# The second MoE weights cast in flight by GpSimd's DMAs, a last store in two halves, and a new order of the work

## The chip, the cores and the metric

The kernel runs on one core of a Trainium2 chip. Its time is the device time of one execution in microseconds (us). The engines that matter: TensorE (PE; PEld are its weight loads), VectorE (DVE), ScalarE (ACT), GpSimd (POOL) and SyncE (SP). In the kernel before, SP issues every DMA. Each engine works through its own instructions in program order and waits on semaphores for the others.

## The reference

The reference is a recurrent attention (RWKV-6) followed by a two-layer MoE block with a squared ReLU, all in float32:

```python
batch, n_heads, seq, head_dim = (4, 8, 768, 48)
for t in range(S):
    cur = einsum('bhd,bhe->bhde', u[None] * kt, vt)
    y[:, :, t] = einsum('bhd,bhde->bhe', rt, state + cur)
    state = wt[:, :, :, None] * state + einsum('bhd,bhe->bhde', kt, vt)
x = y.transpose(0, 2, 1, 3).reshape(3072, 384)
h = x @ w_in            # w_in: 384 x 2048
g = maximum(h, 0) ** 2
out = g @ w_out         # w_out: 2048 x 384
```

## The kernel before, in words

The 4 x 768 tokens are worked in 12 steps of 256 tokens (`T`), three for each batch entry. A step loads its w, r, k and v (384 KB each, `load_step`, line 200), turns the recurrence inside the step into matrix products, carries the state from step to step (`ts_`, `sn_`), and passes its 256 rows through the MoE.

A step s runs like this. `ww_` multiplies neighbouring decays, `lw_` takes logarithms, `cum_` sums them with triangular matmuls into PSUM, `exp_` and `ac_` exponentiate. `rw_` and `kw_` multiply r and k by w, and `rd_` scales them by the decays. `tr_` with `rkt_` (TensorE and a copy) or `dtr_` (a transposing DMA from SP) transposes the result. `p_` forms the products of r and k, `pm_` masks them. `su_` forms the update of the state. `y_`, `yc_` and `yq_` sum three parts of the output in one PSUM bank pair; the last uses `vq_`, made by `ku_`, `qp_` and `vq_` on POOL with `q_` on DVE between. `ysb_` copies the sum, `yt_` with `xt_` (or `dyt_` by DMA) transposes it. `m1_.s.g` is one of eight groups of six matmuls with the first weights; each fills one of four PSUM banks, which `rl_.s.g` (ReLU) reads and frees. `sq_.s.q` squares a quarter of the hidden rows. In steps 0 to 4 `m2_.s.c.q` multiplies a quarter with the second weights, four matmuls a group, and `os_` scales the result out. In steps 5 to 11 a scheme with seven instead of eight block products takes its place: `tw_` forms sums of weight blocks, `sw_` sums of hidden blocks, `pw_.s.1` to `pw_.s.7` are eight matmuls each, `cx_` and `ow_` gather them, and `store` writes 128 rows of the output.

The order of all this isn't made by loops: the string `ORDER` (line 17) lists every operation of all steps as one sequence of words, and the loop at line 634 issues them. Each engine gets its own operations in that order. A word such as `rl_.0.3=V` also says which engine takes it (A is ACT, V is DVE, G is POOL), and `:2` which PSUM bank. So `ORDER` fixes each engine's queue and SP's queue of DMAs too. Which SBUF buffer an operation uses follows from the order as well (`buf`, line 173): a buffer is handed on after a counted number of uses.

The MoE weights come as float32 and are used as float16. `load_wi(g)` and `load_wo(g)` (lines 208 and 213), called by the words `ld.g.i` and `ld.g.o`, let SP load a quarter (768 KB) into one of four staging buffers `w_st`, and `cast` (line 218) copies it into `wi_sb` or `wo_sb`. Quarter q of the second weights is what `m2_.s.c.q` multiplies with; quarter g of the first serves the groups `m1_.s.2g` and `m1_.s.2g+1`. Each staging buffer carries one quarter of the first and one of the second weights; after its last use it becomes output buffers, room for the weight sums, or room for the hidden sums (lines 183 to 191).

Of the kernel before, what the change touches and what calls it, by code (L numbers as in the profile page):

```python
# [22 lines left out]
pm_.1.1 cast.i.1=A yt_.0:3 sn_.0.1 su_.1:0 xt_.0=V qp_.1 ts_.1.0=V m1_.0.1:3 cast.i.2=A pm_.1.0 m1_.0.3:2 m1_.0.0:0  # L23
rl_.0.1=A sn_.1.0 q_.1 ld.2.v cast.i.3=A m1_.0.2:1 rl_.0.3=V m1_.0.4:3 vq_.1 ld.0.o ts_.1.1=V rl_.0.2=A y_.1:1
rl_.0.0=V yc_.1 ld.3.k ww_.2=G yq_.1 m1_.0.5:2 ysb_.1=V ku_.2 m1_.0.6:0 lw_.2 rl_.0.4=V rl_.0.5=A yt_.1:1 sq_.0.0=A
cum_.2:1 ld.1.o xt_.1=V m1_.0.7:3 ld.3.w kw_.2=G rl_.0.6=A m1_.1.1:1 ld.2.o exp_.2 sn_.1.1 m1_.1.4:2 rl_.1.1=V
rl_.0.7=A m1_.1.0:0 rw_.2=G sq_.0.3=A rl_.1.4=V m1_.1.5:1 rl_.1.0=V qp_.2 m1_.1.7:2 rd_.2.0 rl_.1.5=A m1_.1.6:0 ld.3.r
rl_.1.7=A rd_.2.1 tr_.2.0:3 cast.o.0=G rl_.1.6=A m1_.1.2:1 ld.3.o rkt_.2.0=V v_.2=A tr_.2.1:2 rl_.1.2=A m1_.1.3:0
ku_.3 rkt_.2.1=V ac_.2 sq_.1.0=A su_.2:0 q_.2 m2_.0.0.0:1 ld.4.w m2_.0.1.0:3 ts_.2.0=V sq_.0.1=A cast.o.1=G rl_.1.3=V
ld.3.v p_.2.0:1 p_.2.1:0 ww_.3=V sq_.1.1=A m2_.1.1.0:0 vq_.2 m2_.1.0.0:2 pm_.2.1 lw_.3 sq_.1.2=A m2_.0.0.1 pm_.2.0  # L30
m2_.1.1.1 sn_.2.0 sq_.1.3=A m2_.1.0.1 sq_.0.2=V cast.o.2=A m2_.0.1.1 ld.4.k qp_.3 y_.2:1 yc_.2 yq_.2 m2_.1.1.2 kw_.3=G
ld.4.r q_.3 cast.o.3=A cum_.3:0 m2_.0.1.2 ysb_.2=V ww_.4=G m2_.0.0.2 exp_.3 m2_.1.0.2 ac_.3 rw_.3=G lw_.4 rd_.3.1
m2_.1.1.3 v_.3=G m2_.1.0.3 os_.1.1=V dtr_.3.1 cum_.4:1 rd_.3.0 kw_.4=G os_.1.0=A yt_.2:0 exp_.4 m2_.0.0.3 xt_.2=V
ku_.4 dtr_.3.0 ac_.4 m2_.0.1.3 os_.0.0=A rw_.4=V su_.3:0 store.0.0 m1_.2.4:1 ts_.3.0=A ld.4.v rd_.4.1 m1_.2.7:0
# [63 lines left out]
def kernel(  # L98
# [54 lines left out]
    for kind, first in (("r", 0), ("k", 16)):  # L153
# [8 lines left out]
                xT=9, gt=20, o=2, sg=8, xz=6)  # L162
    live, done = {}, {}
    in_halves = {int(word.split(".")[1]) for word in ORDER.split() if word.startswith("rd_.") and word.count(".") == 3}

    def uses_of(kind, key):
        if kind == "S":
            s, c = key
# [443 lines left out]
    def store(s, c):  # L612
        t0 = s * T + c * C
        nc.sync.dma_start(out=out[t0:t0 + C, :], in_=buf("o", s, c)[:])
# [61 lines left out]
```

## Time and profile before

| | us |
|---|---|
| median of 3 runs | 178.47 (177.96 to 178.54) |
| the profiled execution, its own time | 177.58 |
| its span in the profile | 175.8 |
| busy in the span: PE, DVE, ACT, POOL | 169.0, 141.8, 135.4, 125.5 |

The profile is one execution; its times count from the start of the span, and 1.8 us of the execution's time lie outside the span. A row of the timeline gives start, length, engine, line of the code, operation, what it writes `<-` what it reads, shapes and types, and, where the engine stood idle before it, for how long and what released it in brackets. A row of the groups gives the busy time, the mean length in ns of one instruction, and the idle time before them. A row of the stretches gives the busy time of each engine between two times. For a DMA a row gives how long its issue took and the time from issue to landing. A DMA's line is that of its issue: L201 is a load of w, r, k or v, L209 of the first and L214 of the second weights, L614 a store.

### The profile page before, as it was taken

The page shows a single profiled execution, that of the slowest core. Times are in us where ns is not written, and L with a number is a line of the kernel's source. Part 1 is how long each engine was busy: PE and PEld are TensorE (multiplying, and loading weights), DVE is VectorE, ACT ScalarE, POOL GpSimd, SP SyncE. Part 2 cuts the span into 40 slices and gives each one's busy share as a digit, 9 for nine tenths or more (in the row PEclk, how much of TensorE's full clock was granted, in tenths as well). Part 3 has the DMA queues.
Part 4 walks back from the last instruction along what each step waited for, and adds up shares of the span by engine and source line. Part 5 has one row for each costly group of instructions (what it writes and reads, how often), then busy time and mean ns, then how long its engine had stood idle before and what let it go on. Part 6 is the DMA issues. An engine that isn't in the chain of part 4 may idle for free.

```text
span 175.8 us, 5827 instructions
## 1 busy us (share of the span) xinstructions
PE 169.0 (96%) x2431; PEld 133.7 (76%) x2431; DVE 141.8 (81%) x221; ACT 135.4 (77%) x229; POOL 125.5 (71%) x116
## 2 busy tenths in 40 slices
PE   7978899999999999999999999999999999999992
PEld 2346778756686786578876888899988888989991
DVE  5499977996968859987987979969899879788640
ACT  6779798997569878759899799997896778467220
POOL 6398999999597399959999239679948764264320
PEclk9999999999999999999999999999999999999999
DMA  5999999999579999597998969949969710420133
GB/s 148 323 360 383 360 248 365 355 349 260 108 200 316 232 228 265 144 212 195 296 186 224 335 132 246 229 106 303 175 133 158 192 45 4 147 77 4 45 117 111
DMA packets 82523, 36.55 MB, mean 208 GB/s; under 512 B 75841, under 2 KB 80962, under 8 KB 82498
## 3 DMA queue, kind: packets, MB, share of 16 engines
q1 hardware_dynamic: 82498, 36.19, 81.1%
q8 instruction: 19, 0.31, 0.7%
q14 instruction: 6, 0.05, 0.1%
HBM read 25.17 MB, written 4.72 MB: 170 GB/s over the span
## 4 chain that ended last, share of the span: by engine, by line
PE 85%; SPq 5%; DMA 5%; issue 1%; ACT 1%; ACTq 0%
PE one L513 35%; PE one L590 19%; PE one L536 15%; PE att L450 7%; DMA w_st_b<-in_moe_w_in_dram 5%; SPq L201 4%; PE att L404 3%; PE att L426 2%; SPq L209 1%; PE att L334 1%; PE one L496 1%; PE att L336 1%; PE one L379 1%; PE att L332 0%; ACT gt_b L520 0%
## 5 line engine op out<-in xcount | busy, mean ns | idle before, releaser
L513 PE MATMUL one<-xT_b,wi_sb 128*128 128x256 bf16 x576 | 70.2, 273 | 0.5 <-ACT gt_b L520 0.3
L513 PEld LDWEIGHTS <-wi_sb 128*128 128x128 f16 x576 | 54.8, 98 | 9.1 <-issue 1.3
L520 ACT ACTIVATE gt_b<-one 128x512 f16<-128x512 f32 x70 | 40.9, 596 | 10.2 <-PE one L513 9.3
L528 ACT ACTIVATE gt_b<-gt_b 128x1024 bf16<-128x1024 f16 x42 | 43.5, 1056 | 1.4 <-DVE gt_b L522 1.0
L415 DVE TENSOR_TENSOR pmT_b<-att,mask 128x1024 bf16<-128x1024 f32 x22 | 26.3, 1219 | 4.4 <-PE att L404 4.4
L536 PE MATMUL one<-wo_sb,gt_b 128*128 128x384 f16 x160 | 28.7, 326 | 0.0
L590 PEld LDWEIGHTS <-gt_b 128*128 128x128 bf16 x280 | 23.2, 98 | 0.9 <-issue 0.4
L307 POOL TENSOR_TENSOR ku_b<-k_b,u_bc 128x768 f32<-128x768 f32 x12 | 22.0, 1831 | 0.6 <-ACT u_bc L238 0.5
L536 PEld LDWEIGHTS <-gt_b 128*128 128x128 bf16 x160 | 15.1, 98 | 9.6 <-issue 0.5
L312 POOL TENSOR_TENSOR ku_b<-ku_b,r_b 128x768 f32<-128x768 f32 x12 | 22.0, 1831 | 0.2
L440 POOL TENSOR_TENSOR S_b<-t_b,ac_buf 128x384 bf16<-128x384 f32 x20 | 16.8, 841 | 6.1 <-ACT t_b L434 5.4
L522 DVE TENSOR_SCALAR gt_b<-one 128x512 f16<-128x512 f32 x26 | 17.6, 687 | 2.8 <-PE one L513 1.8
L318 POOL TENSOR_TENSOR vq_b<-v_b,q_b 128x768 bf16<-128x768 f32 x12 | 18.2, 1518 | 0.7 <-DVE q_b L315 0.6
L590 PE MATMUL one<-wo_sb,gt_b 128*128 128x192 f16 x168 | 16.2, 246 | 0.0
L370 DVE TENSOR_TENSOR rdec_buf<-r_b,att 128x768 bf16<-128x768 f32 x12 | 11.4, 949 | 2.4 <-POOL r_b L300 1.2
L370 DVE TENSOR_TENSOR rdec_buf<-k_b,att 128x768 bf16<-128x768 f32 x12 | 11.4, 949 | 1.9 <-ACT ac_buf L356 1.5
L595 ACT ACTIVATE w_st_b<-one 128x192 f32<-128x192 f32 x14 | 4.4, 329 | 10.3 <-PE one L590 10.2
L300 POOL TENSOR_TENSOR r_b<-r_b,w_b 128x384 f32<-128x384 f32 x8 | 8.0, 1002 | 5.2 <-DMA r_b<-in_r_dram 5.2
L315 DVE TENSOR_REDUCE q_b<-ku_b 128x16 f32<-128x768 f32 x12 | 11.3, 943 | 0.0
L590 PE MATMUL one<-w_st_b,gt_b 128*128 128x192 f16 x112 | 11.2, 246 | 0.0
L436 DVE TENSOR_TENSOR t_b<-S_b,att 128x384 f32<-128x384 bf16 x16 | 8.8, 549 | 3.0 <-POOL S_b L440 2.5
L288 POOL TENSOR_TENSOR ww_b<-w_b 128x384 f32<-128x384 f32 x7 | 8.1, 1159 | 4.0 <-DMA w_b<-in_w_dram 4.0
(100 smaller groups left out, 268.2 us busy)
## 6 DMA issues: line engine op xcount, KB each, us to landing
w_b<-in_w_dram SPq DMA_DIRECT2D x12, 384.0 KB, 5.7
r_b<-in_r_dram SPq DMA_DIRECT2D x12, 384.0 KB, 5.3
k_b<-in_k_dram SPq DMA_DIRECT2D x12, 384.0 KB, 4.9
v_b<-in_v_dram SPq DMA_DIRECT2D x12, 384.0 KB, 4.6
out_dram<-w_st_b SPq DMA_DIRECT2D x24, 192.0 KB, 2.1
w_st_b<-in_moe_w_in_dram SPq DMA_DIRECT2D x4, 768.0 KB, 8.3
w_st_b<-in_moe_w_out_dram SPq DMA_DIRECT2D x4, 768.0 KB, 8.2
rkT_b<-rdec_buf SPq DMA_TRANSPOSE x18, 3.4
```

Source lines behind the costliest of these rows:

```text
L307: nc.gpsimd.tensor_mul(buf("ku", s)[:], buf("k", s)[:, :, 1:3, :], u_bc[:, :, None, :].to_broadcast([C, H, 2, D]))
L312: nc.gpsimd.tensor_mul(ku[:], ku[:], buf("r", s)[:, :, 0:2, :])
L318: nc.gpsimd.tensor_mul(buf("vq", s)[:].rearrange("p j h d -> p h j d"), buf("v", s)[:], buf("q", s)[:, :, :, None].to_broadcast([C, H, 2, D]))
L370: nc.vector.tensor_mul(rdec[:, i, :, heads, 0:D], x.rearrange("p h j d -> p j h d"), decay[:, None, :, :].to_broadcast([C, 2, n, D]))
L415: nc.vector.tensor_mul(pmT, ps_p[:].rearrange("p e (a x) -> p (e a) x", a=2), mk.to_broadcast([C, 4, 2 * C]))
L440: nc.gpsimd.tensor_mul(buf("S", s + c, 1 - c)[:], buf("t", s, c)[:].rearrange("p (a e d) -> p a e d", a=HP, e=2), tiles["a_c", s][:, :, c, ...
L513: nc.tensor.matmul(ps1[:, j, :], wi_sb[:, n // 4, kk, n % 4 * 128:(n % 4 + 1) * 128], xT[:, :, kk, :], start=(kk == 0), stop=(kk == KT - 1))
L520: nc.scalar.activation(rl, m1, AF.Relu, scale=RS)
L522: nc.vector.tensor_scalar(out=rl, in0=m1, scalar1=RS, scalar2=0.0, op0=ALU.mult, op1=ALU.max)
L528: nc.scalar.activation(gt, rl, AF.Square)
L536: nc.tensor.matmul(m2, gt[:, n, c * C:(c + 1) * C], wo_sb[:, n, :], start=(n == 0), stop=(n == NT - 1))
L590: nc.tensor.matmul(where_to, gt[:, n, :], wo[:, n, :], start=(n == 0 and i in (1, 2, 5)), stop=(n == NT // 2 - 1), skip_group_check=True)
```

## The change

- The second weights are no longer loaded by SP into staging buffers and cast by POOL and ACT. A new operation `gld_(g)` issues from GpSimd's queue a DMA that reads a quarter of the float32 weights from DRAM and writes it as float16 straight into `wo_sb`. There are four of them. The four words `ld.g.o` and the four words `cast.o.g` are gone.
- The staging buffers carry the first weights alone, so they become output buffers and room for sums after one use each (`done` counts 1 to 4 instead of 5 to 8).
- `store` can write one half of the columns. The last store, 11.1, goes as two, `store.11.1.1` (the right half) ahead of store 11.0 and `store.11.1.0` behind it.
- One dummy matmul at the very end (`warm_.1.5`) is gone.
- `ORDER` is new from the first MoE matmul on: the sequence on every engine, the PSUM banks, and for 108 operations the engine. Up to `m1_.0.1` it is unchanged.

The order's part up to step 2, its end, and the code (words that the lists share are on both sides):

```diff
-pm_.1.1 cast.i.1=A yt_.0:3 sn_.0.1 su_.1:0 xt_.0=V qp_.1 ts_.1.0=V m1_.0.1:3 cast.i.2=A pm_.1.0 m1_.0.3:2 m1_.0.0:0
-rl_.0.1=A sn_.1.0 q_.1 ld.2.v cast.i.3=A m1_.0.2:1 rl_.0.3=V m1_.0.4:3 vq_.1 ld.0.o ts_.1.1=V rl_.0.2=A y_.1:1
-rl_.0.0=V yc_.1 ld.3.k ww_.2=G yq_.1 m1_.0.5:2 ysb_.1=V ku_.2 m1_.0.6:0 lw_.2 rl_.0.4=V rl_.0.5=A yt_.1:1 sq_.0.0=A
-cum_.2:1 ld.1.o xt_.1=V m1_.0.7:3 ld.3.w kw_.2=G rl_.0.6=A m1_.1.1:1 ld.2.o exp_.2 sn_.1.1 m1_.1.4:2 rl_.1.1=V
-rl_.0.7=A m1_.1.0:0 rw_.2=G sq_.0.3=A rl_.1.4=V m1_.1.5:1 rl_.1.0=V qp_.2 m1_.1.7:2 rd_.2.0 rl_.1.5=A m1_.1.6:0 ld.3.r
-rl_.1.7=A rd_.2.1 tr_.2.0:3 cast.o.0=G rl_.1.6=A m1_.1.2:1 ld.3.o rkt_.2.0=V v_.2=A tr_.2.1:2 rl_.1.2=A m1_.1.3:0
-ku_.3 rkt_.2.1=V ac_.2 sq_.1.0=A su_.2:0 q_.2 m2_.0.0.0:1 ld.4.w m2_.0.1.0:3 ts_.2.0=V sq_.0.1=A cast.o.1=G rl_.1.3=V
-ld.3.v p_.2.0:1 p_.2.1:0 ww_.3=V sq_.1.1=A m2_.1.1.0:0 vq_.2 m2_.1.0.0:2 pm_.2.1 lw_.3 sq_.1.2=A m2_.0.0.1 pm_.2.0
...
-ow_.11.4=V pw_.11.4 ow_.11.2=V store.11.0 warm_.1.5 ow_.11.3=A store.11.1
+pm_.1.1 cast.i.1=A yt_.0:3 sn_.0.1 su_.1:0 xt_.0=V qp_.1 ts_.1.0=V m1_.0.1:3 cast.i.2=A pm_.1.0 m1_.0.2:0 m1_.0.0:1
+rl_.0.1=A sn_.1.0 q_.1 ld.3.w cast.i.3=A m1_.0.5:2 y_.1:1 vq_.1 ld.2.v ww_.2=V m1_.0.3:3 yc_.1 rl_.0.3=A ld.3.k gld_.0
+yq_.1 rl_.0.0=V lw_.2 m1_.0.4:3 ysb_.1=A ts_.1.1=V m1_.0.7:1 gld_.1 rl_.0.5=V rl_.0.4=A cum_.2:1 rl_.0.7=A ld.4.w
+yt_.1:2 rw_.2=V gld_.2 rl_.0.2=A m1_.0.6:1 xt_.1=V exp_.2 ld.3.r m1_.1.3:3 kw_.2=G rl_.0.6=A rd_.2.0 m1_.1.1:2
+rl_.1.3=A sn_.1.1 m1_.1.6:0 rd_.2.1 rl_.1.1=A m1_.1.0:3 gld_.3 ld.3.v rl_.1.6=V tr_.2.0:1 rl_.1.0=A m1_.1.2:2 v_.2=G
+ld.4.k rkt_.2.0=V sq_.0.1=A m1_.1.7:0 ww_.3=G sq_.1.0=A tr_.2.1:1 rl_.1.7=V m1_.1.4:3 ku_.2 rkt_.2.1=V rl_.1.2=A
+su_.2:0 sq_.0.0=A rl_.1.4=V m1_.1.5:2 ts_.2.0=V m2_.1.1.0:0 qp_.2 rl_.1.5=A m2_.0.1.0:3 ac_.2 sq_.1.1=A m2_.0.1.1
+ku_.3 m2_.0.0.0:1 sq_.0.3=A q_.2 ld.4.r m2_.1.0.0:2 kw_.3=V sq_.1.2=A p_.2.0:1 p_.2.1:0 sn_.2.0 m2_.0.0.1 sq_.0.2=A
+pm_.2.0 m2_.1.1.1 sq_.1.3=A pm_.2.1 m2_.1.0.1 ld.4.v qp_.3 lw_.3 m2_.0.0.2 cum_.3:0 m2_.1.0.2 exp_.3 rw_.3=G m2_.1.1.2
+rd_.3.1 m2_.1.0.3 vq_.2 rd_.3.0 v_.3=A m2_.1.1.3 dtr_.3.1 y_.2:1 q_.3 ww_.4=G ac_.3 yq_.2 yc_.2 os_.1.1=V su_.3:0
...
+pw_.11.3 ow_.11.4=V store.11.1.1 pw_.11.4 ow_.11.2=V store.11.0 ow_.11.3=A store.11.1.0
...
+    in_parts = {tuple(int(x) for x in word.split(".")[1:3]) for word in ORDER.split()
+                if word.startswith("store.") and word.count(".") == 3}
...
+        more += kind == "o" and key in in_parts
...
-            if kind == "w_st" and done[kind] == 5:
+            if kind == "w_st" and done[kind] == 1:
...
-            elif kind == "w_st" and done[kind] in (6, 7):
+            elif kind == "w_st" and done[kind] in (2, 3):
...
-            elif kind == "w_st" and done[kind] == 8:
+            elif kind == "w_st" and done[kind] == 4:
...
-    def load_wo(g):
-        nc.sync.dma_start(
-            out=buf("w_st", "o", g)[:].rearrange("p (a d) -> p a d", d=DM),
+    def gld_(g):
+        nc.gpsimd.dma_start(
+            out=wo_sb[:, g * 4:(g + 1) * 4, :],
             in_=moe_w_out[g * 512:(g + 1) * 512, :].rearrange("(a p) d -> p a d", p=128))
...
-    def store(s, c):
-        t0 = s * T + c * C
-        nc.sync.dma_start(out=out[t0:t0 + C, :], in_=buf("o", s, c)[:])
+    def store(s, c, i=None):
+        t0, cols = s * T + c * C, slice(0, DM) if i is None else half[i]
+        nc.sync.dma_start(out=out[t0:t0 + C, cols], in_=buf("o", s, c)[:, cols])
```

## The prediction

> **What bounds the kernel now.** I read the busy time by stretch first, then the chain that ended last, and then the timeline of the start and the tail, because the first two show that nothing between start and tail can give anything.
>
> ```profile
> 19.00:24.00 5.00, 4.67 (x82) 3.79 (x81) 4.18 (x6) 4.01 (x5) 4.46 (x4) 1.00 1.02 292
> 24.00:172.00 148.00, 148.00 (x2135) 121.28 (x2132) 123.47 (x191) 116.53 (x198) 107.34 (x87) 1.00 0.80 195
> ```
>
> The rows give length, then busy time (instructions) of PE, weight load, DVE, ACT, POOL, then the granted clock, the DMA share and GB/s. From 24 to 172 us TensorE is busy 148.0 of 148 us at clock 1.00. Busy time alone doesn't show that it runs at its pace, so I look at the chain (start, length, what):
>
> ```profile
> 59.97 0.65 PE one L513 x6
> 60.62 0.65 PE one L536 x4
> ...
> 65.09 0.57 PE att L404 x32
> 65.67 0.76 PE one L513 x6
> ...
> 158.45 13.88 PE one L590 x168
> ```
>
> Six matmuls of 256 columns take 0.65, and 168 of 192 columns take 13.88 with no gap. The only loss that repeats is 0.10-0.11 us: the same six take 0.76 after the attention matmuls that use 64 rows. So the end is set by three things: when TensorE starts on the MoE (about 19 us), its work with these switches, and the 3.5 us from the last matmul at 172.3 to the end. The new order holds the same matmuls but one dummy at the end, so the 148 us can only grow: every wait put ahead of TensorE there is paid in full, and there are no waits to win back.
>
> **The change, part by part.** The sum is made against the profiled execution (177.58 us, span 175.8) and carried to the median of the runs, 178.47, which is 0.9 above it.
>
> *Casts and engines.* Two casts of 1.46 leave POOL and two leave ACT; 108 operations change between ACT, DVE and POOL. I cost that at nothing: beside TensorE's 148.0 us the row has DVE 123.5, ACT 116.5 and POOL 107.3, so TensorE's work covers them, as long as no single one comes late.
>
> *Switches.* Counting in the two orders how often TensorE goes from 128-row work into a group of 64-row work after its first MoE matmul, I get 26 before and 28 after: 2 x 0.10 = +0.2.
>
> *The start.* Up to the first MoE matmul the orders are equal, so these rows still hold:
>
> ```profile
> 19.04 2.78 PE L513 MATMUL one<-xT_b,wi_sb 128*128 128x256 bf16 x24 [0.20 <-DVE xT_b L500]
> 22.10 0.82 PE L513 MATMUL one<-xT_b,wi_sb 128*128 128x256 bf16 x6 [0.29 <-ACT gt_b L520]
> ...
> 26.19 4.75 PE L513 MATMUL one<-xT_b,wi_sb 128*128 128x256 bf16 x42
> ```
>
> ```profile
> 20.08 1.47 ACT L221 CAST wi_sb<-w_st_b 128x1536 f16<-128x1536 f32 x1 [0.89 <-DMA w_st_b<-in_moe_w_in_dram]
> ```
>
> Before, four groups of six run from 19.04 and the fifth waits 0.29 until 22.10. After, the fourth group is `m1_.0.5`, which needs the third cast of the first weights, done at 20.08 + 1.47 = 21.55; it starts at 21.6 and ends at 22.26, 0.16 later than the same amount of work before. With one of the two extra switches (`m1_.0.3` now splits `y_.1` from `yc_.1`), TensorE is through step 0 at 26.19 + 0.66 + 0.26 = 27.1 instead of 26.85.
>
> The next group needs `xt_.1` on DVE, and DVE's queue is where the change bites: `ww_.2` and `rw_.2` now stand on it, ahead of `xt_.1`, and both wait for loads.
>
> ```profile
> 20.58 0.94 DVE L315 TENSOR_REDUCE q_b<-ku_b 128x16 f32<-128x768 f32 x1
> ...
> 26.03 0.56 DVE L500 COPY xT_b<-one 128x768 bf16<-128x768 bf16 x1 [0.25 <-PE one L496]
> ```
>
> ```profile
> 21.60 1.47 POOL L318 TENSOR_TENSOR vq_b<-v_b,q_b 128x768 bf16<-128x768 f32 x1 [0.32 <-DVE q_b L315]
> 23.29 1.00 POOL L288 TENSOR_TENSOR ww_b<-w_b 128x384 f32<-128x384 f32 x1 [0.21 <-DMA w_b<-in_w_dram]
> ```
>
> ```profile
> L522 DVE TENSOR_SCALAR gt_b<-one 128x512 f16<-128x512 f32 x26 | 17.6, 687 | 2.8 <-PE one L513 1.8 <-ACT gt_b L520 0.6
> L436 DVE TENSOR_TENSOR t_b<-S_b,att 128x384 f32<-128x384 bf16 x16 | 8.8, 549 | 3.0 <-POOL S_b L440 2.5 <-PE att L426 0.5
> L300 DVE TENSOR_TENSOR r_b<-r_b,w_b 128x384 f32<-128x384 f32 x4 | 3.2, 808 | 0.5 <-DMA r_b<-in_r_dram 0.5
> L288 DVE TENSOR_TENSOR ww_b<-w_b 128x384 f32<-128x384 f32 x5 | 2.8, 556 | 1.0 <-DMA w_b<-in_w_dram 1.0
> ```
>
> DVE is free at 21.52 and waits for w of step 2, whose landing released POOL at 23.29. Then 23.29 + 0.56 (`ww_.2`) + 0.69 (`rl_.0.0`) + 0.55 (`ts_.1.1`) + 0.69 (`rl_.0.5`) = 25.8; `rw_.2` 0.81 makes 26.6, `xt_.1` 0.56 makes 27.15: TensorE, ready at 27.1, waits 0.1 at most. Behind `rw_.2` on DVE stand `xt_.1` and with it all of step 1's matmuls, so any lateness of r of step 2 after 25.8 is TensorE's.
>
> *That load, and the new queue.* Landings (k and r of step 2, from issue):
>
> ```profile
> L201 SPq DMA_DIRECT2D k_b<-in_k_dram x1: 4342/4342/4342, 13.6 to 13.6; - x1
> DMA to landing us min/median/max: 10.7/10.7/10.7
> L201 SPq DMA_DIRECT2D r_b<-in_r_dram x1: 3968/3968/3968, 18.0 to 18.0; - x1
> DMA to landing us min/median/max: 7.6/7.6/7.6
> ```
>
> k lands at 24.3 and r at 25.6, so r's transfer fills 1.3 us; the DMA share in 19-24 is 1.02, nothing is spare. Before, the second weights stand behind these loads in SP's one queue:
>
> ```profile
> q1 hardware_dynamic: 82498, 36.19, 81.1%
> ```
>
> ```profile
> L201 SPq DMA_DIRECT2D v_b<-in_v_dram x1: 1082/1082/1082, 22.0 to 22.0; - x1
> DMA to landing us min/median/max: 5.8/5.8/5.8
> L214 SPq DMA_DIRECT2D w_st_b<-in_moe_w_out_dram x4: 1022/2034/2256, 23.2 to 31.3; - x4
> DMA to landing us min/median/max: 6.7/8.2/8.3
> ```
>
> After, `gld_.0` comes from POOL once `vq_.1` ends at 23.07. (The least values, 1.02 and 6.7, are the first weight load's.) What POOL pays for an issue no row shows; the nearest are these issues of the same transfers from SP, 1.02 for the first and up to 2.26 for those behind a full queue. POOL's queue is its own and empty, so I take 1.1, and keep nothing and 2.26 as the ends. The Trainium skill (DMA: Bandwidth & Descriptors, Specifications) gives about 1 us to the first byte for a DMA issued from GpSimd, which would leave the sum as it is. So the weights start at 24.2, beside r. How two queues share the engines no row shows either: from no delay (r first) to all of the first weights first. I take half each: r needs 2.6 instead of 1.3 us, lands at 26.9, and DVE's `rw_.2` starts 1.1 later than 25.8: +1.1.
>
> *POOL's own queue.* Before, `vq_.2` ends at 35.22 + 1.79 = 37.0 and is used at 40.46.
>
> ```profile
> 28.87 1.81 POOL L312 TENSOR_TENSOR ku_b<-ku_b,r_b 128x768 f32<-128x768 f32 x1
> 30.62 1.47 POOL L221 CAST wo_sb<-w_st_b 128x1536 f16<-128x1536 f32 x1
> ...
> 35.22 1.79 POOL L318 TENSOR_TENSOR vq_b<-v_b,q_b 128x768 bf16<-128x768 f32 x1
> ```
>
> ```profile
> 40.46 0.36 PE L450 MATMUL att<-vq_b,ident 64*64 64x384 bf16 x4
> ```
>
> After, four issues (4.4), `v_.2`, `sn_.2.0` (0.8 each) and `qp_.3` (1.8) come ahead of it and two casts (2.9) go: 37.0 + 4.9 = 41.9. TensorE has five more groups of second-weight matmuls ahead of that use (0.65 each, 3.3) and comes 0.26 later out of the start; `cum_.3` comes in and `yc_.2` goes behind, which cancel: about 44.0. A margin of 2.1, so cost nothing. If it is gone, `yq_.2` stands on TensorE and waits. Halved loads (2.6 us each) bring w of step 3 to 29.5 and v of step 2 to 32.1, where POOL, through with its issues at about 29.3, would wait for `v_.2`; that eats most of the margin. The weights themselves, 2.1 us each alone (v of step 2 lands at 27.8, the first of them at 29.9), 4.2 halved, are all there by 24.2 + 16.8 = 41.0; the last is first read some 2 us ahead of `yq_.2`, at 42. Hidden too, with 1 us to spare.
>
> *SP's queue* loses four issues of 1.02 to 2.26, and the loads of steps 3 and 4 move up past them, w of step 3 ahead of v of step 2, v of step 4 ahead of the first transposes of step 3. They are issued earlier and then wait in the DMA queue; apart from r and v of step 2 no user of theirs is early enough to notice. No gain: TensorE never waited for them.
>
> *The tail.* The last store goes in two halves, the right one ahead of store 11.0.
>
> ```profile
> 173.00:174.00 1.00, 0.00 (x0) 0.00 (x0) 0.00 (x0) 0.00 (x0) 0.00 (x0) 1.00 0.85 306
> ```
>
> ```profile
> DMA to landing us min/median/max: 1.9/2.1/6.4
> ```
>
> The last two stores, 192 KB each, mostly move in this microsecond; 96 KB of it would be gone earlier, at 306 GB/s 0.3 us. The gain lies between nothing (no store landed under 1.9 us) and half a landing, 1.05. I take -0.3. The dummy matmul that goes lay beside the last product: nothing.
>
> **Sum:** start +0.16 +0.1 (wait for `xt_.1`), switches +0.2, r late +1.1, tail -0.3: +1.26, so 178.47 + 1.26 = 179.7.
>
> **The rivals.**
> *A, r isn't late:* the first weights come in only after r has landed. Then +0.16, 178.6, no change. For it: the weights' first byte and r's last are only 1.4 us apart. Against: the DMA share is full.
> *B, turns go by packets, not bytes:* a row of a step load is 384 B, one of the weights 1536 B. r's 64 rows per engine took 1.3 us, 20 ns each; a weight's 32 took 2.1, 66 ns. Alternating, r needs 64 x 86 ns = 5.5 us, lands at 29.7, and the wait is 3.9: 182.5. The Trainium skill (DMA: Bandwidth & Descriptors, Queues, rings and completion order) says that an engine goes round its queues by packets; no row here shows two busy queues.
> *C, POOL is held by the issues:* decides from about 1.6 us apiece, where 4 x 0.5 eats the margin of 2.1 before `yq_.2`. At 2.26 apiece POOL is 4.6 later and TensorE waits 2.5, 181.2 with r on time; at 3, 5.5, 184.1. Against: 1.02 for the same transfer from SP. For it: DVE and POOL already hold each other up, one square on DVE taking 2.24 instead of 0.68 while POOL worked on one of its L312 products.
>
> ```profile
> L530 DVE TENSOR_TENSOR gt_b<-gt_b x6: 678/686/2242, 37.9 to 155.4; 128x1024 bf16<-128x1024 f16 x6
> ```
>
> The Trainium skill (SBUF — State Buffer, SBUF: two separate sides) states that a DVE operation in a two-port mode keeps GpSimd from writing the descriptors of its DMA. By that an issue could last one such operation longer, 0.68, which four times is 2.7 and past the margin; but the order has no 16-bit operation between SBUF tiles on DVE until the issues are done, so I leave C at 0.09.
>
> *D, faster:* the last store's small half lands in 1.05 instead of 2.1 and r is on time: 0.46 - 1.05 = -0.6, 177.9. It decides below a landing of about 1.1 us. Against: 1.9 was the shortest of 24.
>
> **How the numbers follow.** Forecast 0.38, A 0.27, B 0.15, C 0.09, D 0.11. A measurement tells 0.3% (0.5 us) from no change here. Slower is the forecast, B and C: 0.62; same is A: 0.27; faster is D: 0.11. The range starts at D's 177.9 and reaches beyond B to 183.0, leaving out C's far end and some of D.
>
> **What would show it.** Right: DVE's `rw_.2` waits for r's DMA around 26-27, TensorE has a gap of about 1 us before the first matmul of step 1, and none over 0.2 after it; a second DMA queue carries 3.1 MB. Wrong: `rw_.2` starts by 25.8 (A), the gap is 4 us (B), or it sits ahead of `yq_.2` near 44 with POOL late (C). A gap elsewhere between 45 and 172 would be one that I haven't seen: I followed the new order instruction by instruction only to there.

## The result, and the profile after

The changed kernel takes 185.49 us (median; 183.53 to 189.58), the kernel before 178.5 on the same chip: a ratio of 1.034, interval 1.028 to 1.040. The forecast was 179.7 with a range of 177.9 to 183.0: the right side, but a sixth of the loss (1.2 of 7 us). The profiled execution is the longest of those, 189.58 us with a span of 187.7, 11.9 more than before's 175.8, so its waits are likely larger than the usual ones. The granted clock, averaged over each of the four executions, was 0.98, 0.98, 0.98 and 0.99.

The busy time by stretch of the changed kernel (length, then busy time and instructions of PE, weight load, DVE, ACT, POOL, then granted clock, DMA share, GB/s):

```profile
24.00:36.00 12.00, 11.30 (x152) 9.42 (x153) 8.42 (x13) 11.01 (x18) 4.91 (x6) 1.00 1.12 196
36.00:43.00 7.00, 2.05 (x15) 1.54 (x15) 0.97 (x2) 0.69 (x1) 2.92 (x3) 0.77 1.13 264
43.00:48.00 5.00, 5.00 (x21) 2.45 (x19) 2.15 (x2) 4.78 (x8) 4.92 (x4) 0.64 1.08 293
48.00:184.00 136.00, 135.53 (x2006) 110.81 (x2005) 111.94 (x178) 101.33 (x170) 97.72 (x81) 1.00 0.75 160
```

From 48 us on TensorE is busy 135.5 of 136 us, as before. The loss sits ahead of that: 5 us of idle time between 36 and 43, and a clock of 0.77 and 0.64 where the kernel before had 1.00 throughout. 6.8 us at half clock in a span of 187.7 give a mean of 0.982; by that estimate the other three executions had a stretch at half clock too, two of about this length and one of half of it. TensorE's timeline there, and POOL's:

```profile
34.77 0.82 PE L516 MATMUL one<-xT_b,wi_sb 128*128 128x256 bf16 x6
40.95 0.80 PE L429 MATMUL att<-v_bf_b,rdec_buf 64*128 64x96 bf16 x8 [5.36 <-POOL v_bf_b L299]
41.68 1.46 PE L516 MATMUL one<-xT_b,wi_sb 128*128 128x256 bf16 x6
42.94 5.24 PE L539 MATMUL one<-wo_sb,gt_b 128*128 128x384 f16 x20
```

```profile
23.94 2.43 POOL L217 DMA_DIRECT2D wo_sb<-in_moe_w_out_dram  x3
27.08 0.99 POOL L307 TENSOR_TENSOR k_b<-k_b,w_b 128x384 f32<-128x384 f32 x1 [0.71 <-DMA k_b<-in_k_dram]
28.04 0.82 POOL L443 TENSOR_TENSOR S_b<-t_b,ac_buf 128x384 bf16<-128x384 f32 x1
28.82 0.81 POOL L217 DMA_DIRECT2D wo_sb<-in_moe_w_out_dram  x1
40.08 0.82 POOL L299 CAST v_bf_b<-v_b 128x768 bf16<-128x768 f32 x1 [10.46 <-DMA v_b<-in_v_dram]
40.88 0.98 POOL L291 TENSOR_TENSOR ww_b<-w_b 128x384 f32<-128x384 f32 x1
```

POOL comes to `v_.2` at 29.6 and waits 10.46 us for v of step 2; `su_.2`, the first to use it, waits 5.36 us on TensorE. Behind the wait six matmuls of 256 columns take 1.46 us instead of 0.82 and twenty of 384 columns 5.24. SyncE's issues of w of step 3 and v of step 2, at 24.6 and 25.7 us, and their landing (the least time is w's, the greatest v's):

```profile
L204 SPq DMA_DIRECT2D w_b<-in_w_dram x1: 1073/1073/1073, 24.6 to 24.6; - x1
L204 SPq DMA_DIRECT2D v_b<-in_v_dram x1: 1160/1160/1160, 25.7 to 25.7; - x1
DMA to landing us min/median/max: 12.4/13.3/14.3
```

They land at 37.0 and 40.0, where v took 5.8 us before. In the meantime two queues work on the same 16 DMA engines, which move their bytes in packets; here a packet is about one row (2112 packets for the 2048 rows of the second weights), 384 B of a step load or 1536 B of the weights. The packets from 31 to 34 us (packets, MB, share of the 16 engines; q0 is GpSimd's queue, q1 SyncE's):

```profile
q0 software_dynamic: 542, 0.40, 85.8%
q1 hardware_dynamic: 540, 0.21, 38.9%
```

The counts are equal, as with one packet each in turn: 34 pairs per engine in 3 us, 88 ns a pair. Rival B had 20 + 66 = 86. So SyncE's queue moves 70 GB/s here, with 134 of weights as written, instead of the 292 that it had alone from 19 to 24 us in the kernel before. The turns aren't even from the start: from 28 to 29 us GpSimd's queue moved 266 packets and SyncE's none, though w was issued at 24.6 (in the second run of the changed kernel 274 to 3, from 30 to 31). Why isn't known; here it adds about 1 us to the lateness.

The length splits so: the first MoE matmul starts at 19.95 (before 19.04), +0.91; from there to the last matmul's end at 184.72 it takes 164.77 instead of 153.28, +11.49; from there to the end of the span 2.98 instead of 3.48, -0.50. Of the 11.49, 5.36 are the wait, some 2.8 the low clock behind it (0.80, 1.46 and 5.24 against 0.50, 0.83 and 3.41 for the same groups in a run below with the clock at 1.00), 2.0 waits for the casts of the first weights, whose loads came late in this execution, and the rest smaller waits that I haven't split. DVE, where the forecast had its wait, shows this:

```profile
25.77 0.56 DVE L291 TENSOR_TENSOR ww_b<-w_b 128x384 f32<-128x384 f32 x1 [3.33 <-DMA w_b<-in_w_dram]
28.23 1.05 DVE L303 TENSOR_TENSOR r_b<-r_b,w_b 128x384 f32<-128x384 f32 x1 [0.24 <-DMA r_b<-in_r_dram]
```

`rw_.2` waited 0.24 us for r, not 1.1.

### The profile page after: what moved, and what is told of

Same layout as the page of the kernel before. It is cut to its first block, busy times and chain, and to the rows that moved or that the text cites. A ratio compares the mean times of both kernels' runs of the same rounds, so it can differ in the third digit from the quotient of the medians.

```text
span 187.7 us, 5815 instructions
## 1 busy us (share of the span) xinstructions
PE 172.4 (92%) x2430; PEld 134.6 (72%) x2430; DVE 140.5 (75%) x222; ACT 134.3 (72%) x223; POOL 128.4 (68%) x121
## 3 DMA queue, kind: packets, MB, share of 16 engines
q0 software_dynamic: 2112, 1.57, 5.4%
## 4 chain that ended last, share of the span: by engine, by line
PE 38%; DVE 4%; POOL 3%; DMA 3%; issue 1%; ACT 1%; POOLq 0%
PE one L593 17%; PE one L516 15%; PE att L453 3%; DMA v_b<-in_v_dram 3%; PE att L407 1%; DVE pmT_b L418 1%; PE att L429 1%; POOL S_b L443 1%; DVE gt_b L525 1%; POOL w_st_b L571 1%; POOL r_b L303 1%; DVE q_b L318 1%; POOL k_b L307 1%; DVE w_st_b L558 1%; DVE t_b L439 0%
## 5 line engine op out<-in xcount | busy, mean ns | idle before, releaser
L516 PE MATMUL one<-xT_b,wi_sb 128*128 128x256 bf16 x576 | 71.7, 274 | 2.2 <-ACT wi_sb L224 2.0
L523 ACT ACTIVATE gt_b<-one 128x512 f16<-128x512 f32 x69 | 40.0, 596 | 19.2 <-PE one L516 18.6
L531 ACT ACTIVATE gt_b<-gt_b 128x1024 bf16<-128x1024 f16 x44 | 45.3, 1054 | 0.2
L539 PE MATMUL one<-wo_sb,gt_b 128*128 128x384 f16 x160 | 30.5, 341 | 0.0
L593 PEld LDWEIGHTS <-gt_b 128*128 128x128 bf16 x280 | 23.3, 98 | 0.7 <-issue 0.2
L539 PEld LDWEIGHTS <-gt_b 128*128 128x128 bf16 x160 | 15.8, 102 | 10.6 <-issue 1.7
L525 DVE TENSOR_SCALAR gt_b<-one 128x512 f16<-128x512 f32 x27 | 18.3, 684 | 2.2 <-PE one L516 1.9
L318 DVE TENSOR_REDUCE q_b<-ku_b 128x16 f32<-128x768 f32 x12 | 11.3, 945 | 4.1 <-POOL ku_b L315 4.1
L571 POOL TENSOR_TENSOR gt_b<-gt_b,w_st_b 128x512 bf16<-128x512 bf16 x7 | 8.2, 1180 | 8.9 <-PE one L593 8.9
L303 POOL TENSOR_TENSOR r_b<-r_b,w_b 128x384 f32<-128x384 f32 x10 | 10.1, 1010 | 4.4 <-DMA r_b<-in_r_dram 4.4
L352 ACT ACTIVATE att<-att 128x768 f32<-128x768 f32 x12 | 9.6, 798 | 4.9 <-PE att L339 4.5
L429 PE MATMUL att<-v_bf_b,rdec_buf 64*128 64x96 bf16 x160 | 6.4, 207 | 6.1 <-POOL v_bf_b L299 5.4
## 6 DMA issues: line engine op xcount, KB each, us to landing
w_st_b<-in_moe_w_in_dram SPq DMA_DIRECT2D x4, 768.0 KB, 11.1
```

The source lines that it names most:

```text
L516: nc.tensor.matmul(ps1[:, j, :], wi_sb[:, n // 4, kk, n % 4 * 128:(n % 4 + 1) * 128], xT[:, :, kk, :], start=(kk == 0), stop=(kk == KT - 1))
L523: nc.scalar.activation(rl, m1, AF.Relu, scale=RS)
L525: nc.vector.tensor_scalar(out=rl, in0=m1, scalar1=RS, scalar2=0.0, op0=ALU.mult, op1=ALU.max)
L531: nc.scalar.activation(gt, rl, AF.Square)
L539: nc.tensor.matmul(m2, gt[:, n, c * C:(c + 1) * C], wo_sb[:, n, :], start=(n == 0), stop=(n == NT - 1))
L593: nc.tensor.matmul(where_to, gt[:, n, :], wo[:, n, :], start=(n == 0 and i in (1, 2, 5)), stop=(n == NT // 2 - 1), skip_group_check=True)
```

## The experiments

The theory after this reading: GpSimd's queue takes every other turn of the DMA engines with packets four times as large, for some 10 us, and the new order lets work stand behind the loads that this starves. Rivals: the cast in flight itself is slow; the new order costs the time without the DMAs; the low clock has a cause of its own.

### The changed kernel again

> The changed kernel once more, unchanged. Theory P (turns by packets): while the second weights are in POOL's DMA queue, each DMA engine gives SP's queue one 384 B packet for each 1536 B packet of the weights, so v of step 2 lands about 10 us later than before and TensorE stands about 5 us ahead of su_.2; that comes again, and so does a lower clock behind the gap. Open: the waits of 1.5 and 0.6 us for the casts of the first weights near 20-24 us; if they belong to the change they come again, if only to that execution they don't. 183 to 186 us.

183.89 us (180.40 to 185.06), ratio 1.035 (1.028 to 1.042). The profiled execution is the shortest, 180.4, and has no gap:

```profile
25.69 2.42 POOL L217 DMA_DIRECT2D wo_sb<-in_moe_w_out_dram  x3
30.67 0.83 POOL L299 CAST v_bf_b<-v_b 128x768 bf16<-128x768 f32 x1
```

Here the first MoE matmul comes at 21.46, 2.4 us later than in the kernel before, and POOL is late with it, while SyncE issued its loads as early as ever (v at 23.6, and at 25.7 in the first profile): v had landed before the GpSimd DMAs filled the turns. From the first MoE matmul to the last it took 154.2 us, 0.9 more than before. So the size of the loss depends on which queue comes first, by 2 us. The late start is TensorE's: up to about 14 us its matmuls take twice as long (four dummies 1.91 us, in the kernel before 1.02), though the clock's column reads 1.00 there. That stretch lies ahead of everything that the change touches, and a run further down in the order of the kernel before starts the same way; its cause is open. Of the nine executions of the changed kernel so far, this is the only one whose mean clock is 1.00; the others have 0.98 or 0.99.

### The parts apart

The DMAs alone, in the order of the kernel before:

```diff
-ld.0.o ... ld.1.o ... ld.2.o ... ld.3.o ... cast.o.0=G ... cast.o.1=G ... cast.o.2=A ... cast.o.3=A
+gld_.0 ... gld_.1 ... gld_.2 ... gld_.3
```

> The order of before with only the weights' path changed: the four loads become casting DMAs from POOL at their old places in the order, the four casts go. Theory P: v of step 2 is the second load behind the start of the weights and lands at about 35 to 37 instead of 27.8; it is wanted at 31.5, so TensorE stands 3 to 5 us ahead of su_.2: 181 to 185. Rival O: 178 to 179.5.

179.72 us, ratio 1.010 (1.007 to 1.013): a miss, and above the rival's 179.5 too. In that order v of step 2 stands right behind r in SyncE's queue and lands early; the only wait of over 0.6 us on TensorE comes from POOL:

```profile
26.75 0.80 POOL L218 DMA_DIRECT2D wo_sb<-in_moe_w_out_dram  x1
27.58 1.01 POOL L308 TENSOR_TENSOR k_b<-k_b,w_b 128x384 f32<-128x384 f32 x1
28.52 0.80 POOL L218 DMA_DIRECT2D wo_sb<-in_moe_w_out_dram  x1
29.34 0.85 POOL L444 TENSOR_TENSOR S_b<-t_b,ac_buf 128x384 bf16<-128x384 f32 x1
30.14 1.00 POOL L304 TENSOR_TENSOR r_b<-r_b,w_b 128x384 f32<-128x384 f32 x1
```

```profile
32.19 0.62 PE L383 MATMUL one<-ident,rdec_buf 128*128 128x128 bf16 x8 [1.34 <-DVE rdec_buf L374]
```

`rw_.2` starts at 30.14 instead of 27.91, behind three issues of 0.80 to 0.94 us. The issues here go out at 23.1, 26.8, 28.5 and 32.9, not three in 2.4 us.

The order alone, with the weights by SyncE and four casts put back at places of my choice:

```diff
-gld_.0 ... gld_.1 ... gld_.2 ... gld_.3
+ld.0.o ... ld.1.o ... ld.2.o ... ld.3.o
+cast.o.0=G (ahead of m2_.1.1.0)  cast.o.1=G (ahead of m2_.0.1.1)  cast.o.2=A (behind sq_.0.2)  cast.o.3=A (behind sq_.1.3)
```

> The new order alone: the second weights go back into SP's one queue (at the places of the four gld words) and are cast by POOL and ACT (two each), with the staging buffers used twice as before. Theory P: v of step 2 lands by about 30, no gap over 0.5 us ahead of su_.2; the casts may cost up to 2 us at the first second-weight matmuls; 178.5 to 181. Rival O (the new order itself is what costs, with w of step 3 ahead of v of step 2 and tighter queues on DVE): 183 or more.

183.56 us, ratio 1.032 (1.026 to 1.039): by the number the rival's, as slow as the changed kernel. But no gap stands ahead of `su_.2`. The longest wait is for a cast that I put in on POOL, and the next, 1.46 us ahead of `cum_.3`, for ACT, which was held by another of them, so this run doesn't price the order:

```profile
37.30 2.11 PE L545 MATMUL one<-wo_sb,gt_b 128*128 128x384 f16 x12 [1.94 <-POOL wo_sb L230]
```

The same with the four loads issued by GpSimd, staged in fp32 and not cast in flight:

```diff
-        nc.sync.dma_start(out=buf("w_st", "o", g)...
+        nc.gpsimd.dma_start(out=buf("w_st", "o", g)...
```

> As the new order alone, but the four loads of the second weights are issued from POOL, still float32 into staging buffers and cast by POOL and ACT: POOL's queue without the cast in flight. Theory P: v of step 2 lands at 37 to 41 as in the changed kernel, 183 to 188. Rival K (the cast in flight makes those transfers slow, and that is what holds the others up): near the new order alone, under 181.

190.12 us (189.49 to 191.10), ratio 1.068 (1.062 to 1.074), above the 183 to 188 expected, with the gap in it. The second pair of rows is its packets from 31 to 34 us:

```profile
39.57 0.80 PE L435 MATMUL att<-v_bf_b,rdec_buf 64*128 64x96 bf16 x8 [5.48 <-POOL v_bf_b L305]
```

```profile
q0 software_dynamic: 256, 1.01, 90.4%
q1 hardware_dynamic: 257, 0.09, 12.8%
```

In the edit only the issuing queue differs from the run before. So GpSimd's queue makes the gap, and the cast in flight isn't needed for it. Without the cast that queue's packets are larger, 3.15 MB in 768, some 4 KB each: again one for one, but a pair takes 187 ns, and SyncE's queue is down to 30 GB/s. The whole time isn't to be set against the changed kernel's, since the casts are waited for here too (1.94 and 0.46 us).

### The packet's size

```diff
-        nc.gpsimd.dma_start(out=wo_sb[:, g * 4:(g + 1) * 4, :], in_=...)
+        for cols in half:
+            nc.gpsimd.dma_start(out=wo_sb[:, g * 4:(g + 1) * 4, cols], in_=...[..., cols]...)
```

> Each of the four GpSimd DMAs goes in two of half the columns: the same bytes in reads of 768 B instead of 1536 B, twice as many packets, eight issues. Theory (two queues on an engine take turns by packets): from 31 to 37 us the two queues still have equal counts of packets, but a turn takes 20 + 33 ns instead of 20 + 66, so w of step 3 and v of step 2 land about 4 us sooner, v at 35 to 36 instead of 40.0; 182 to 185 us with the wait in. Rival (turns by bytes, or SyncE's queue simply waits until GpSimd's has drained): v at 39 to 41 as before, and the longer issuing on POOL adds up to 3 us: 186 to 191 us.

181.77 us, ratio 1.016 (1.010 to 1.023). The packets from 34 to 37 us:

```profile
q0 software_dynamic: 774, 0.29, 77.5%
q1 hardware_dynamic: 774, 0.29, 56.2%
```

Still one for one, and so on to 43 us, but a pair takes 62 ns instead of 88, and SyncE's queue gets 0.29 MB in 3 us instead of 0.20. From 31 to 34 us it was 931 to 657. So once both queues are under way the turns go by packets: equal counts with three sizes, at 62, 88 and 187 ns a pair. The time isn't as clean a proof: this profile's execution is one with the late start (21.51), and eight issues held POOL longer, so v was there when POOL came to it.

### Which load is late, and who stands behind it

v of step 2 ahead of w of step 3:

```diff
-ld.3.w cast.i.3=A m1_.0.5:2 y_.1:1 vq_.1 ld.2.v
+ld.2.v ld.3.w cast.i.3=A m1_.0.5:2 y_.1:1 vq_.1
```

> One exchange in SyncE's queue: v of step 2 goes out ahead of w of step 3. Theory (the loads of SyncE's queue lose turns to GpSimd's DMAs, and v of step 2 is hurt because it stands behind w of step 3): v lands at 27 to 32 us, the 5.4 us gap ahead of su_.2 goes, and so does the low clock behind it; 180.0 to 181.5 us. A smaller wait may stay for w of step 3, which then lands at 37 or later: POOL waits for it in ww_.3 with qp_.2 and vq_.2 behind it. Rival (GpSimd's DMAs starve every load of that stretch, the order in SyncE's queue is no matter): v still lands at 38 or later, 184 to 189 us.

184.22 us, ratio 1.031 (1.023 to 1.039), a miss (180.0 to 181.5 expected). v is there at 29.1, the gap ahead of `su_.2` is gone, and the wait has moved to w of step 3, which POOL wants next:

```profile
29.09 0.82 POOL L299 CAST v_bf_b<-v_b 128x768 bf16<-128x768 f32 x1 [0.48 <-DMA v_b<-in_v_dram]
35.02 0.99 POOL L291 TENSOR_TENSOR ww_b<-w_b 128x384 f32<-128x384 f32 x1 [5.12 <-DMA w_b<-in_w_dram]
```

TensorE waits 3.65 us later on, in front of `cum_.3`, and the clock falls behind that too. Next I also moved that product on POOL behind step 2's own work:

```diff
-v_.2=G ... ww_.3=G ... ku_.2 ... qp_.2
+v_.2=G ... ku_.2 ... qp_.2 ww_.3=G
```

> The changed kernel with v of step 2 ahead of w of step 3 in SyncE's queue, as in the run that did this alone (where POOL then waited 5.12 us for w in ww_.3, and TensorE 3.65 us for pm_.2), and ww_.3 moved on POOL from ahead of ku_.2 to behind qp_.2, so that step 2's products don't stand behind that wait. Theory (the loads are late by the shared turns, but the price is set by what stands behind the wait on POOL): pm_.2 no longer waits, ku_.3 and vq_.2 behind ww_.3 come at about 36 + 3.6, no single wait on TensorE above 1.5 us, the clock stays at 1.00; 180 to 181.5 us. Rival (every order pays the lateness of some load): a wait of 3 us or more in another place, 182.5 to 185 us.

183.99 us, ratio 1.030 (1.024 to 1.036): my theory's number missed, its rival's came. The wait for w is 1.97 now, and k of step 3, third in the line of starved loads, holds both engines:

```profile
34.92 1.00 POOL L291 TENSOR_TENSOR ww_b<-w_b 128x384 f32<-128x384 f32 x1 [1.97 <-DMA w_b<-in_w_dram]
39.78 1.81 POOL L310 TENSOR_TENSOR ku_b<-k_b,u_bc 128x768 f32<-128x768 f32 x1 [3.87 <-DMA k_b<-in_k_dram]
39.81 2.20 DVE L307 TENSOR_TENSOR k_b<-k_b,w_b 128x384 f32<-128x384 f32 x1 [4.49 <-DMA k_b<-in_k_dram]
```

TensorE waits 3.42 us for `pm_.2` behind that DVE product. So the lateness isn't v's own: each load that SyncE's queue has open in that stretch is late.

All four DMAs behind `v_.2`:

```diff
-gld_.0 ... gld_.1 ... gld_.2 ... gld_.3 ... v_.2=G
+v_.2=G gld_.0 gld_.1 gld_.2 gld_.3
```

> The four GpSimd DMAs are issued behind v_.2 on POOL, so they start once v of step 2 has landed, and nothing but w of step 3 and what follows competes with them. Theory: w of step 3 and v of step 2 land by 29, no gap ahead of su_.2, clock 1.00; the weights land from 32 to 42 us, the first read m2_.1.1.0 stands behind su_.2 at about 35 and may wait up to 1 us, m2_.0.0.x follow; 178.3 to 181 us. Rival (the DMAs cost the same wherever they stand, because they move the same bytes in a stretch whose share is full): the wait goes to the second weights or to the k and r loads of step 3, 3 us or more: 182 to 186 us.

183.56 us, ratio 1.028 (1.018 to 1.038), again the rival's number. v lands at 28.7 and no gap stands ahead of `su_.2`, but now the weights themselves are late:

```profile
36.69 1.47 PE L539 MATMUL one<-wo_sb,gt_b 128*128 128x384 f16 x8 [2.35 <-DMA wo_sb<-in_moe_w_out_dram]
39.62 2.11 PE L539 MATMUL one<-wo_sb,gt_b 128*128 128x384 f16 x12 [1.45 <-DMA wo_sb<-in_moe_w_out_dram]
```

### The low clock

Dummy matmuls on TensorE ahead of `su_.2`, thirteen and then twenty-two:

```diff
-su_.2:0
+warm_.13.4 su_.2:0        (second run: warm_.22.4)
```

> Thirteen dummy matmuls of 0.38 us ahead of su_.2 keep TensorE busy for 5 us while it would wait for v. Theory (the low clock of 36 to 48 us in the changed kernel follows from TensorE's idle time): in an execution in which the wait is there, the clock stays at 1.00 from 36 to 48 us, the 20 matmuls of 384 columns that took 5.16 us take 3.25, and the time is 2 to 2.5 us less than 189.6. In an execution in which v is in time the dummies cost 5 us. Rival (the low clock comes from something else, such as the load of all engines after the wait): the clock is below 0.8 there all the same and the time doesn't fall.

> As the run with thirteen dummy matmuls ahead of su_.2, but with twenty-two (8.4 us): there 3.07 us of idle time were left and the clock still fell to 0.62 from 40 to 44 us. Theory (the clock falls behind an idle stretch of about 3 us or more): no idle time over 0.5 us is left, the clock stays at 1.00 from 36 to 48 us, and the 20 matmuls of 384 columns behind take 3.25 us instead of 5.16 (3.94 with thirteen). Rival (the clock falls through something that happens at that place whether TensorE is idle or not): below 0.8 again. The time itself can rise by up to 3 us, since the dummies also run where v comes in time.

In the profile of thirteen 3.07 us of waiting were left; with twenty-two, none. The first two rows are of the run with thirteen, the next two of the run with twenty-two:

```profile
39.87 0.79 PE L430 MATMUL att<-v_bf_b,rdec_buf 64*128 64x96 bf16 x8 [3.07 <-POOL v_bf_b L300]
41.85 4.01 PE L540 MATMUL one<-wo_sb,gt_b 128*128 128x384 f16 x20
```

```profile
39.85 3.41 PE L540 MATMUL one<-wo_sb,gt_b 128*128 128x384 f16 x20
40.00:46.00 6.00, 6.00 (x67) 3.62 (x65) 2.65 (x3) 5.92 (x9) 5.92 (x4) 1.00 1.04 277
```

From 40 to 46 us the clock was 0.50 in the changed kernel, 0.75 with thirteen dummies, 1.00 with twenty-two, and the twenty matmuls took 5.24, 4.01 and 3.41 us. So the low clock follows from TensorE's idle time. The times stay, 184.25 (ratio 1.028, 1.020 to 1.036) and 184.21 (1.033, 1.028 to 1.039): the twenty-two dummies take 4.91 us themselves, about what the wait took, and a wait of 1.30 for `pm_.2` follows. These two runs also show the late load away from the longest execution: up to `su_.2` their order is the changed kernel's, and v lands at 39.0 and 37.9 us.

### The turns taken away, and spread out

The changed kernel without the second weights' loads, the array set to zero at the start, so the result lacks the second product while TensorE does the same matmuls:

```diff
-gld_.0 ... gld_.1 ... gld_.2 ... gld_.3
...
+        for g in (0, 1):
+            nc.vector.memset(wo_sb[:, g * 4:(g + 1) * 4, :], 0.0)
...
+        for g in (2, 3):
+            nc.gpsimd.memset(wo_sb[:, g * 4:(g + 1) * 4, :], 0.0)
```

> The changed kernel without the loads of the second weights: the four GpSimd DMAs are left out and the array they fill is set to zero at the start, so the product with the second weights is left out of the result; TensorE does the same matmuls. Theory (what the change costs is the four DMAs' turns on the engines): v of step 2 lands by 29, no wait over 1 us ahead of TensorE after 24 us, clock 1.00; 177.5 to 179 us. Rival (the new order of the other work costs most of it, whatever the DMAs do): waits of 3 us or more in all stay in the stretch from 24 to 172 us; 181 to 184 us.

179.95 us, ratio 1.009 (1.005 to 1.013), above my 179. The trace says where that is:

```profile
21.94 2.23 PE L520 MATMUL one<-xT_b,wi_sb 128*128 128x256 bf16 x19 [0.20 <-DVE xT_b L507]
```

```profile
24.00:36.00 12.00, 12.00 (x165) 9.97 (x163) 9.14 (x15) 10.54 (x16) 11.05 (x9) 1.00 1.05 276
36.00:48.00 12.00, 12.00 (x165) 7.52 (x164) 7.95 (x11) 9.08 (x16) 10.04 (x9) 1.00 0.26 59
```

The first MoE matmul is at 21.94, 2.9 us later than before. About 1.0 of this is there at the first matmuls of `cum_` (6.45 instead of 5.42 us), behind the zeroing; the rest comes with the late start of the second run of the changed kernel (the four dummies take 1.91 us here too). From there TensorE has no wait to 48 us, and to its last matmul 154.09 us pass, 0.8 more than before, 0.71 of it in one wait near 102 us. So in this execution the new order by itself costs about 0.8 us. By the medians 2.0 of 7.0 us stay without the DMAs, the start included, and the other 5 come with them: their turns, the waits and the low clock behind them, and POOL's 3 us of issues, which this run leaves out too. Seven of the ten executions have a mean clock of 0.98 or 0.99, and none of those was profiled, so some low clock comes without the DMAs, at a place that I don't know.

The DMAs spread out, with v first:

```diff
-gld_.0 ... gld_.1 ... gld_.2 ... gld_.3 ... v_.2=G ... ww_.3=G
+gld_.0 ... sn_.1.1 gld_.1 ... v_.2=G gld_.2 ... ww_.3=G gld_.3
```

> The changed kernel with v of step 2 ahead of w of step 3, and the four GpSimd DMAs spread out on POOL: the first where it is, the second behind sn_.1.1, the third behind v_.2, the fourth behind ww_.3, so that about 3 us lie between issues (as in the order of the kernel before, where they went out at 23.1, 26.8, 28.5 and 32.9 us). Theory (it is the bunch of three issues in 2.4 us that fills the engines' other turns for 10 us): the wait of POOL for w of step 3 falls from 5.1 to 2 us or less, k of step 3 lands before 37, TensorE's longest single wait after 24 us is under 2 us and the clock stays at 1.00; 179.5 to 181.5 us. Rival (each 1536 B row takes its turn wherever it goes out, so the sum of the lateness stays): waits of 4 us or more in all, on the loads or on the weights themselves; 182.5 to 185 us.

181.34 us, ratio 1.016 (1.010 to 1.021). The time is as expected: half the loss goes. The clock at 1.00 that I expected with it didn't come. What is left are waits for v (2.90 us on POOL), for r of step 3, and 1.86 us of TensorE for `vq_.2` behind it, after which the clock falls once more:

```profile
43.51 1.81 POOL L315 TENSOR_TENSOR ku_b<-ku_b,r_b 128x768 f32<-128x768 f32 x1 [2.92 <-DMA r_b<-in_r_dram]
```

### The last store, and the DMAs in the order of the kernel before

The kernel before with the last store in two halves, and nothing else:

```diff
-store.11.0 warm_.1.5 ow_.11.3=A store.11.1
+store.11.1.1 (behind ow_.11.4) ... store.11.0 ow_.11.3=A store.11.1.0
```

> The kernel before with one change: the last store goes in two halves of the columns, the right half ahead of store 11.0, the left half last (the dummy matmul ahead of the last product goes too). Theory (the prediction's tail step, and what the changed kernel's own end shows: 2.98 us from the last matmul to the end of the span instead of 3.47): 0.3 to 0.5 us less than before, 177.9 to 178.2. Rival (the end of a store is its fixed landing time, whatever its size): within 0.1 us of before.

177.50 against 177.81 us, ratio 0.999 (0.997 to 1.001). From the last product to the end of the span it is 3.2 us instead of 3.5. The sign is as expected; the interval doesn't tell it from nothing.

The same tail on the run of the DMAs alone, with two issues moved behind `rw_.2`:

```diff
-gld_.1 ... kw_.2=G ... gld_.2 ... rw_.2=G
+kw_.2=G ... rw_.2=G gld_.1 gld_.2
```

> The second weights by the four GpSimd DMAs in the order of the kernel before, as in the run that did this alone, but the second and third DMA are issued behind rw_.2 on POOL instead of ahead of kw_.2 and rw_.2; the last store in two halves. Theory (what the DMAs cost in the order of before is the 1.34 us that tr_.2.0 waited because POOL came to rw_.2 2.2 us later by three issues of 0.8): that wait falls to 0.2 or less, and with the tail's 0.4 the time is 177.9 to 178.6. Rival (the DMAs cost by the engines' shared bandwidth, so another wait takes its place): a wait of 1 us or more for w of step 3 or for the weights, 179 to 180.5.

180.68 us (178.77 to 190.60), ratio 1.009 (1.005 to 1.014), a miss (177.9 to 178.6 expected). The 1.34 us wait is gone, but the executions scatter. The profiled one is the longest, and has a DVE product of 11.13 us; the same form takes 0.56 elsewhere:

```profile
37.38 11.13 DVE L296 TENSOR_TENSOR ww_b<-w_b 128x384 f32<-128x384 f32 x1
```

```profile
41.73 0.98 POOL L312 TENSOR_TENSOR k_b<-k_b,w_b 128x384 f32<-128x384 f32 x1
```

```profile
36.00:48.00 12.00, 5.82 (x64) 3.28 (x62) 12.00 (x4) 2.37 (x3) 12.00 (x10) 0.86 0.81 142
```

POOL is busy 12.00 of these 12 us, ten instructions without a gap, and the product ends 0.4 us after the last of them. The product wasn't waiting for w of step 3, at least from 41.73 on: `kw_.3` on POOL reads the same w there, in its usual 0.98 us. Then that product on POOL:

```diff
-ww_.3=V
+ww_.3=G
```

> The run with the DMAs in the order of the kernel before and the split last store, with one product moved: ww_.3 from DVE to POOL. There, in the profiled execution of 190.6 us, this product took 11.13 us on DVE instead of 0.56, from 37.38 until POOL's back-to-back work ended at 48.1, and the executions lay between 178.8 and 190.6. Theory (a DVE product of two SBUF operands doesn't get through while POOL works without a gap): with it on POOL no execution is over 181, and the median falls to 178 to 179.3. Rival (the product waited for its data, w of step 3, and the profile counts that as its time): the same lateness stays, now as a wait on POOL; median 180 to 181 with executions above 186.

177.69 us (177.44 to 185.24), against 177.98: ratio 0.997 (0.994 to 1.001). Eleven of twelve executions lie under 178.7. In the profiled one v, w and the weights come in time, and TensorE is at work throughout:

```profile
24.00:172.00 148.00, 147.84 (x2130) 120.95 (x2127) 125.86 (x189) 113.72 (x196) 108.22 (x90) 1.00 0.83 184
```

So four GpSimd DMAs with a cast in flight can stand in this kernel at no cost, and with no gain that these runs can tell. I expected no execution above 181; the one at 185.24 wasn't profiled, and its cause is open.

## Why the prediction was wrong, step by step

- **What bounds the kernel:** right. TensorE had no wait to win back, and every variant is between equal and slower.
- **The start, +0.16:** the casts of the first weights are waited for, as said; in the runs whose first MoE matmul comes at 18.9 to 19.4 TensorE waits 0.35 to 0.9 us for them in all, in the profiled execution 2.0, and that one starts 0.9 late as well.
- **r of step 2 late, +1.1:** wrong. `rw_.2` waited 0.24, in the other profiles of this order at most 0.44. I had the weights start at 24.2, right after an issue of 1.1; the issue does take 0.75 to 0.94, but the first packets of GpSimd's queue appear only from 26 to 27 us, nearly 3 us after the issue began at 23.94. r lands at 28.2 with about 1 us of shared turns.
- **v of step 2 and w of step 3, at nothing: the step that failed.** "Halved loads (2.6 us each) bring w of step 3 to 29.5 and v of step 2 to 32.1 ... that eats most of the margin." They landed at 37.0 and 40.0. With turns by packets a pair takes 88 ns, and the 64 + 64 rows of the two loads 11.3 us of it. I had this as rival B, with 86 ns, but priced it for r alone; the same 86 ns put on the two loads behind r would have given 11.0 us. And I measured v's lateness against `yq_.2` at 44 us, though `su_.2` uses it first: TensorE is ready for that at 35.6 here, POOL's `v_.2` takes 0.8, so whatever v lands behind 34.8 is paid in full. At 32.1 it would have cost nothing; at 40.0 it cost 5.36, and 2.8 of slow clock behind it.
- **SP's queue, "no user of theirs is early enough to notice":** wrong for w, k and r of step 3, each of which became the late one in a run that moved the loads or the DMAs (5.12, 4.49 and 2.92 us).
- **The clock:** no step of the sum had it. About 2.8 us of the profiled execution come from TensorE running at half clock behind a wait of its own.
- **POOL held by the issues (rival C, from 1.6 us apiece):** not in the changed kernel. In the order of the kernel before 0.8 apiece was enough, because I set the price by `yq_.2` and not by `rw_.2`, which three issues made 2.2 us late.
- **Casts, engines and switches, +0.2:** not told apart; together with every other effect of the order behind the start 0.8 us in the profile without the DMAs.
- **The tail, -0.3:** 0.5 less in the changed kernel's profile, 0.3 in the run of it alone, not told from nothing.

The chance of 0.62 for slower was on the right side, but that was luck as far as the sum goes: 1.1 of its 1.26 us came from r, which wasn't late. The range failed at the one term where a rival's mechanism applied to more loads than I had put it on.

## What to carry to other kernels

A second DMA queue isn't a second set of engines: here it took every other packet, and with packets four times as large it left the first queue about a quarter of the rate that it has alone (70 of 292 GB/s). Before a load is moved to it, follow every load that the first queue has open in that stretch to its first user, and spread the issues; bunched, they starve even loads that were issued before their own packets began to flow. And price a wait of 3 us or more on TensorE at one and a half times its length or more, since here the clock was halved behind each of them (5.36 us of wait brought 2.8 us of slow work; 3.07 brought 1.5, by the same three groups).

## What the runs showed of the hardware that I hadn't expected

**GpSimd's DMA starts late.** The first packets come some 2 to 3 us after the start of the issue (issued at 23.94, first seen from 26.5 to 27; at 25.69 in the second run, from 28.0 to 28.5; at 29.45 in the run with the DMAs behind `v_.2`, from 32.0 to 32.5). The Trainium skill (DMA: Bandwidth & Descriptors, Specifications) gives about 1 us to the first byte; here the measurement decides.

**Turns by packets.** 542 against 540 packets, 774 against 774 with half the size, and 256 against 257 with the larger ones of the run without the cast; not where GpSimd's packets set in (266 against 0). The Trainium skill (DMA: Bandwidth & Descriptors, Queues, rings and completion order) says that an engine goes round its queues packet by packet; the equal counts agree, the first microseconds don't.

**Half clock after a wait.** Single waits of TensorE of 5.36, 3.65, 3.42 and 3.07 us each brought a clock of 0.50, for 6.8 us (from 39.9 to 46.6 in the changed kernel), 6.8, 6.9 and 3.5 us; those of 5.48 (with one of 1.94 behind it) and 9.01 us, in the staged run and in the one with the long DVE product, for 10.4 us. Waits of 2.35 and 1.45 us left it at 1.00, but one of 1.86 between attention matmuls, in the run with the DMAs spread, was followed by 3.5 us at 0.50, so the length of the wait alone doesn't decide. The Trainium skill (TensorE: Matmul & The Clock Gate, The HAM clock gate) says that a free-running window of about 3.4 us in which TensorE idles halves the clock; low stretches of 3.5, 6.8 and 10.4 us, one, two and three such windows, agree, while drops after 3.07 and 1.86 us, both shorter than a window, are more than it states.

**A DVE product that doesn't get through.** 11.13 us for 0.56 us of work while POOL ran ten instructions without a gap. The Trainium skill (SBUF — State Buffer, SBUF: two separate sides) says that a DVE operation with two SBUF inputs and a GpSimd operation exclude each other for the length of an instruction; here DVE lost not one but all of ten turns. One execution shows this, the longest of its run, and moving the product to POOL agrees with it; that POOL holds DVE off by this means is argued, not shown.
